# A retention and mixture-of-experts kernel: the first nine chunks computed whole instead of in halves

## The chip, the cores and the metric

The kernel runs on one core of a Trainium2 chip. The metric is the device time of one execution in microseconds (us); the median of three runs of the kernel before is 444.45 us (443.77 to 444.71). The first matrix dimension of a tile lies on up to 128 partitions. TensorE multiplies (PE in the profile, its weight loads PEld), VectorE (DVE) and ScalarE (ACT) work elementwise and read TensorE's result banks, GpSimd (POOL) makes some elementwise products and scatters rows by index, and SyncE (SP) issues most transfers.

## The reference

There are two stages. Retention takes q, k and v of 4 batches, 8 heads, 768 steps and 64 features. The result y is then regarded as 3072 tokens of 512 features, and each token goes to one of 8 experts:

```python
for t in range(S):
    state = gamma * state + einsum('bhd,bhe->bhde', k[:, :, t], v[:, :, t])
    y[:, :, t] = scale * einsum('bhd,bhde->bhe', q[:, :, t], state)
...
logits = x @ w_gate + modality_bias[modality_id]
e_idx = argmax(logits, axis=1)
...
h = maximum(x[mask] @ w1[e], 0.0)
out[mask] = gate_w[mask, None] * (h @ w2[e])
```

Each expert has w1 of 512 x 1024 and w2 of 1024 x 512. All data are float32.

## The kernel before, in words

*Chunks.* Retention works on 24 chunks of 128 tokens, `n` = 0 to 23, six for each batch. The growth of gamma is put into v ahead of time (`decay_v`, on GpSimd, makes the tile vd) and into the result afterwards (`gain`), so that a chunk needs four groups of matmuls: scores (sc, k times q), a masked copy of them on VectorE (a), the growth of the state (st, k times vd, which adds up in one bank over a batch) with a copy of the state by ScalarE (s), and the result y, which is state times q and a times vd. All are plain float32, and the trace shows two records for each such matmul.

*Halves.* Each chunk is worked in two halves of 64 tokens, with 8 heads, so that every operand is 64 x 64 and four matmuls lie in the four quarters of TensorE's array. `scores`, `heads_out` and `grown` make lists of matmuls, `run` issues two lists turn by turn, two matmuls of each, and `quarters(n)` puts them in order: the second half of chunk n's state and chunk n+1's scores beside chunk n's y, with one `yield` in the middle. The v and k of a chunk are laid out for this on the host (`toks`), and so are the factors `dec`.

*Tokens.* ScalarE copies y into yT. One chunk later `tokens_out` turns it and multiplies it with the gate's weights in one group of matmuls (x, 128 x 144), and VectorE and ScalarE make token rows (xs) and logits of it. Every three chunks are a group. `route` puts a group's steps into the list `todo`: choosing experts (`route_a`, which ends in cnt and crep), counting ranks (pc and rk on TensorE), then the scatter of the rows into x_dram by GpSimd. For some groups, the first of them group 1 (chunks 3 to 5), further steps (pk, pt) make a list of two jobs, each a full slot of 256 rows of one expert. Group 0 gives a guess of the first expert (totg), whose weights are loaded ahead.

*The order.* `everything` drives all this. Each time that the generator `retention` yields, `tick` issues one step of `todo`. In before a chunk yields twice. Once the first list exists, the rows and weights of the first job are loaded (the weights only if the guess was wrong), and a counter `ahead` runs down with the yields. When it is 1, the rows are flipped (xp, `flip_x`, with xTh and xTl as high and low parts) and the first quarter of w1 is split into hi (ScalarE, a cast) and lo (VectorE, a difference) by `cut`; at 0 the second quarter is split, and the jobs begin in the middle of chunk 9. From there on `run_job` issues the matmuls of the jobs (h_e with w1, o_e with w2, in three products of high and low parts) and takes a piece of retention at every third step. That part of the order is the same in both kernels.

*The engines' queues.* The order on TensorE, ScalarE, VectorE and SyncE is the order in which the program is written. An instruction that waits holds up all behind it on its engine.

Of the kernel before, what the change touches and what calls it, by code (L numbers as in the profile page):

```python
# [7 lines left out]
F32 = mybir.dt.float32  # L8
# [4 lines left out]
ALU = mybir.AluOpType  # L13
AX = mybir.AxisListType

P = 128
# [5 lines left out]
GRP = 3  # L22
# [11 lines left out]
UNIT = 32  # L34
NTAIL = 2
NUNIT = 144
DENSE = 9
EMPTY = 2 * NCAND
ZROW = NE * NT

# [3 lines left out]
FC = DF // P  # L44
QW = KC * 256

C_ID, C_MASK, C_DEC, C_IOTA, C_OUT, C_HALF, C_END = 0, 128, 256, 304, 312, 360, 424


@with_exitstack  # L50
def kernel(
# [23 lines left out]
    def bank(name):  # L75
        return ps.tile([P, 512], F32, tag="bank", name=name)
# [42 lines left out]

    gain = cst[:, C_OUT : C_OUT + NCH * H].rearrange("p (c h) -> p c h", h=H)  # L120
    half = cst[:, C_HALF : C_HALF + D]

    tbias = cp.tile([P, NN, NE], F32, name="tbias")
    iota3 = cp.tile([P, GRP, NE], F32, name="iota3")
# [139 lines left out]

    def quarters(n):
        more = 0 <= n and (n + 1) % NCH
        ys = []
        if n >= 0:  # L270
            py = bank(f"y_{n}").rearrange("p (g t) -> p g t", g=NG)
            ys = heads_out(n, py)
# [10 lines left out]
        if n >= 0:  # L283
            yield n
# [6 lines left out]
        if n < 0:  # L291
            return None
# [5 lines left out]
        nc.scalar.copy(yT, py)  # L298
        return yT
# [599 lines left out]
    def flip_x(s):  # L899
        s["xT"] = transpose_x(s["tag"], s["xg"])  # L900
# [43 lines left out]

    def decay_v(n):
        vv = kvs[n][:, 1].rearrange("p (h e) -> p h e", h=H)
        vds[n] = wk.tile([P, H, D], F32, tag="vd", name=f"vd_{n}", bufs=3)
        ins = nc.gpsimd.tensor_tensor(  # L948
            vds[n], vv, dec[:, n % NCH].unsqueeze(2).to_broadcast([P, H, D]), op=ALU.mult
        )  # L950
        vd_last[:] = [getattr(ins, "ins", ins)]

# [60 lines left out]
                todo.extend([lambda e=e: pad_c(e) for e in range(NE)])  # L1013

    def retention(modi):
        list(quarters(-1))
        masked(0)
        decay_v(1)
        setup_a()
        prev = None  # L1020
        for n in range(NN):
            yT = yield from quarters(n)
            if n + 1 < NN:
                masked(n + 1)
            if n + 2 < NN:
                decay_v(n + 2)

            load_kv(n + 7 if n < 3 else n + 3)
            load_kq(n + 8 if n < 4 else n + 4)
            if n == 0:  # L1030
                setup_b(modi)
            elif n == 1:
                list_consts()
            if prev is not None:
                tokens_out(*prev)
                if n % GRP == 0:
                    route(n // GRP - 1)
            prev = (n, yT)
            if n in (GRP - 1, (min(EVENTS) + 1) * GRP - 1):

                tokens_out(*prev)
                route(n // GRP)
                prev = None
            yield n
        tokens_out(*prev)
        route(NGRP - 1)
        yield NN

    def everything():
        load_kq(1)  # L1050
        load_kv(1)
        nc.sync.dma_start(wgt[:, :, P:], wgate)
# [12 lines left out]

        ahead = guess = None
        for n in ret:
            tick()
            if guess is None and "guess" in lists:
                guess = dict(e=reg(lists["guess"], 0, NE - 1))  # L1070
                raw(guess, 1)
                raw(guess, 2)
            if ahead is None:
                if min(EVENTS) in lists:
                    job = state_of[0] = start_job(jobs[0])
                    rows_in(job)
                    raw(job, 1, guess)
                    raw(job, 2, guess)
                    ahead = 2 * (DENSE - n)
            else:  # L1080
                ahead -= 1
                if ahead == 1:
                    flip_x(job)
                    cut(job, 1, 0)
                if ahead == 0:
                    cut(job, 1, 1)
                    break
        for k in range(len(jobs)):
            for t, _ in enumerate(run_job(k)):
                if t % 2:  # L1090
                    tick()
                if t % 3 == 1:
                    next(ret, None)
                if (k, t) in steps:
                    u = steps[k, t]
                    if u not in units:
                        at = 3 * NFIN + u
                        lst = lists["final"]
                        units[u] = unit(
                            f"u{u}", reg(lst, at + U, NE - 1), reg(lst, at, NCAND * UPS)  # L1100
                        )
                    next(units[u], None)
        assert next(ret, None) is None and not todo
# [18 lines left out]
def _layout(inputs):  # L1122
    import numpy as np

    f = np.float32
    q, k, v = inputs["q"], inputs["k"], inputs["v"]

    def feat(a):
        a = a.transpose(0, 1, 3, 2).reshape(B, NG, P, NCH, P)
        return a.transpose(0, 3, 2, 1, 4).reshape(NN, P, DM)  # L1130

    def toks(a):

        a = a.reshape(B, NG, 2, NCH, 2, D, D).transpose(0, 3, 2, 5, 4, 1, 6)
        return a.reshape(NN, P, DM)
# [7 lines left out]
    cst[:, C_DEC : C_DEC + NCH * H] = dec.reshape(P, NCH * H)  # L1143
    cst[:, C_IOTA : C_IOTA + NE] = np.arange(NE)
# [6 lines left out]
    cst[:, C_HALF:] = np.tile(np.triu(np.ones((D, D))), (2, 1))  # L1151
# [25 lines left out]
    return {n: np.ascontiguousarray(a) for n, a in arrs.items()}  # L1177
# [35 lines left out]
```

## Time and profile before

| | |
|---|---|
| median of three runs | 444.45 us (443.77 to 444.71) |
| the profiled execution | 440.58 us |
| its span, first to last instruction | 438.5 us |
| mean granted clock of TensorE | 0.967 |
| instructions | 13128 |
| TensorE busy | 402.6 us, 92% of the span, 5156 matmul records |
| VectorE, ScalarE, GpSimd busy | 242.8, 208.1, 101.9 us |
| moved by DMA | 92.83 MB, mean 212 GB/s |

A line of the timeline gives the start in us, the length in us, engine, line, operation and tiles, the count of merged records, and in brackets the idle time before it with what ended it. Lines of waits give the total, the number of times and the longest. Lines of windows give a stretch, its length, the busy us of each engine with its count, the granted clock, the share of the DMA engines and GB/s. "issue" means that the engine waited for nothing that the profile shows. The profiled execution lies 3.87 us below the median of the runs.

### The profile page before, as it was taken

How to read it: one execution, taken by the hardware profiler on the slowest of the kernel's cores; microseconds unless marked ns; L12 is line 12 of the kernel's file. 1: busy time of each engine (PE TensorE's matmuls, PEld its weight loads, DVE VectorE, ACT ScalarE, POOL GpSimd, SP SyncE). 2: the span in 40 equal slices, each digit the busy share in tenths (PEclk: the TensorE clock that was granted, in tenths of full speed). 3: DMA queues.
4: the chain of work that ended last, by engine and by line, in shares of the span. 5: the costliest groups of instructions: out<-in, count | busy, mean ns of one | idle time of the engine just before them, and what ended most of it. 6: DMA issues, size and time to landing. Idle time of an engine off the chain costs nothing.

```text
span 438.5 us, 13128 instructions
## 1 busy us (share of the span) xinstructions
PE 402.6 (92%) x5156; PEld 352.2 (80%) x5156; DVE 242.8 (55%) x581; ACT 208.1 (47%) x419; POOL 101.9 (23%) x130
## 2 busy tenths in 40 slices
PE   3777788999999998999999999999999999999990
PEld 3766677878988987988888988989898898869850
DVE  1452738756656647745754765887565664635400
ACT  1331436636447555446445636645454646445310
POOL 2423312152132024021311131030486101001010
PEclk9885989999999999999999999999999999999996
DMA  8999639985967682345770224662253999995000
GB/s 287 384 386 301 218 118 305 357 271 207 323 209 243 230 314 90 116 162 178 245 277 25 76 77 165 217 194 73 92 175 117 338 343 356 332 400 222 2 24 20
DMA packets 30895, 92.83 MB, mean 212 GB/s; under 512 B 5550, under 2 KB 5678, under 8 KB 30832
## 3 DMA queue, kind: packets, MB, share of 16 engines
q1 hardware_dynamic: 25360, 77.83, 51.4%
q0 software_dynamic: 5184, 13.67, 8.3%
q8 instruction: 41, 0.67, 0.7%
q10 hardware_dynamic: 288, 0.48, 0.3%
q14 instruction: 22, 0.18, 0.1%
HBM read 94.81 MB, written 17.21 MB: 255 GB/s over the span
## 4 chain that ended last, share of the span: by engine, by line
PE 58%; issue 14%; DMA 3%; DVE 3%; ACT 2%; POOL 2%; SPq 1%; POOLq 0%; ACTq 0%
PE o_e L784 21%; PE h_e L769 21%; PE x L308 4%; PE h_s L769 3%; PE sc L263 3%; PE st L263 2%; PE y L263 2%; DVE lo_e L715 2%; DMA wa_u<-in_w_dram 2%; PE xp_e L754 1%; DMA kq<-in_qkv_dram 1%; ACT hi_e L713 1%; POOL out_dram L797 1%; DMA xg_e<-x_dram 1%; PE uh_u L838 0%
## 5 line engine op out<-in xcount | busy, mean ns | idle before, releaser
L715 DVE TENSOR_TENSOR lo_e<-raw,hi_e 128x1024 fp32r<-128x1024 f32 x80 | 99.3, 1241 | 70.1 <-ACT hi_e L713 64.9
L769 PE MATMUL h_e<-xTh,hi_e 128*128 128x256 f32 x320 | 92.2, 288 | 0.9 <-ACT hi_e L713 0.9
L769 PE MATMUL h_e<-xTh,lo_e 128*128 128x256 f32 x320 | 90.5, 283 | 0.9 <-DVE lo_e L715 0.9
L769 PE MATMUL h_e<-xTl,hi_e 128*128 128x256 f32 x320 | 90.5, 283 | 0.0
L713 ACT CAST hi_e<-raw 128x1024 fp32r<-128x1024 f32 x80 | 83.8, 1047 | 0.0
L784 PE MATMUL o_e<-hi_e,hTh 128*128 128x512 f32 x160 | 66.2, 414 | 0.0
L784 PE MATMUL o_e<-lo_e,hTh 128*128 128x512 f32 x160 | 63.3, 396 | 0.0
L784 PE MATMUL o_e<-hi_e,hTl 128*128 128x512 f32 x160 | 63.1, 394 | 0.0
L769 PEld LDWEIGHTS h_e<-xTh,hi_e 128*128 128x128 f32 x320 | 61.2, 191 | 1.9 <-ACT hi_e L713 1.1
L769 PEld LDWEIGHTS h_e<-xTh,lo_e 128*128 128x128 f32 x320 | 61.2, 191 | 1.4 <-DVE lo_e L715 1.1
L769 PEld LDWEIGHTS h_e<-xTl,hi_e 128*128 128x128 f32 x320 | 61.2, 191 | 0.0
L948 POOL TENSOR_TENSOR vd<-kv,cst 128x512 f32<-128x512 f32 x24 | 26.8, 1117 | 115.6 <-PE y L263 54.8
L722 ACT ACTIVATE hTh<-h_e 128x256 fp32r<-128x256 f32 x80 | 30.5, 387 | 35.3 <-PE h_e L769 30.0
L263 PE MATMUL sc<-kq 64*64 64x64 f32 x768 | 37.4, 239 | 9.0 <-DMA kq<-in_qkv_dram 5.3
L723 DVE SCALAR_TENSOR_TENSOR hTl<-h_e,hTh 128x256 fp32r<-128x256 f32 x80 | 33.2, 419 | 21.1 <-ACT hTh L722 19.8
L258 ACT COPY s<-st 128x256 f32<-128x256 f32 x44 | 16.5, 375 | 58.4 <-PE y L263 31.2
L797 POOL DMA_INDIRECT out_dram<-o_e,xg_e x20 | 20.7, 1035 | 92.1 <-ACT o_e L796 86.2
L263 PEld LDWEIGHTS sc<-kq 64*64 64x64 f32 x768 | 30.7, 149 | 11.0 <-DMA kq<-in_qkv_dram 5.3
L330 ACT ACTIVATE xs<-x,cst 128x64 f32<-128x64 f32 x96 | 22.2, 315 | 33.9 <-issue 24.6
L414 POOL DMA_INDIRECT x_dram<-xs,pos x24 | 25.6, 1067 | 49.2 <-DVE xs L380 22.2
L263 PE MATMUL st<-vd,kv 64*64 64x64 f32 x704 | 33.3, 240 | 3.2 <-ACT s L258 1.1
L784 PEld LDWEIGHTS o_e<-lo_e,hTh 128*128 128x128 f32 x160 | 30.1, 188 | 7.3 <-DVE lo_e L715 0.3
(181 smaller groups left out, 707.0 us busy)
## 6 DMA issues: line engine op xcount, KB each, us to landing
raw<-in_w_dram SPq DMA_DIRECT2D x104, 512.0 KB
kv<-in_qkv_dram SPq DMA_DIRECT2D x24, 512.0 KB
kq<-in_qkv_dram SPq DMA_DIRECT2D x23, 512.0 KB
xg_e<-x_dram SPq DMA_DIRECT2D x20, 257.0 KB
wa_u<-in_w_dram SPq DMA_DIRECT2D x8, 512.0 KB
wb_u<-in_w_dram SPq DMA_DIRECT2D x16, 256.0 KB
xg_s<-x_dram SPq DMA_DIRECT2D x4, 257.0 KB
x_dram<-xs,pos POOLq DMA_INDIRECT x24
```

The costliest lines, as they stand in the source:

```text
L263: nc.tensor.matmul(out_, l, r, start=start, stop=True, skip_group_check=True)
L308: nc.tensor.matmul(px[:, g], yT[:, 2 * u + g], wgt[:, 2 * u + g], start=(g == 0), stop=(g == 1), skip_group_check=True,)
L330: nc.scalar.activation(x[:, i], px[:, i // 2, rows(i % 2)], AF.Copy, scale=gain[:, c, 4 * u + i : 4 * u + i + 1],)
L414: ins = nc.gpsimd.indirect_dma_start(out=x_dram[:, :], out_offset=bass.IndirectOffsetOnAxis(ap=pos[:, i : i + 1], axis=0), in_=xs, in_offs ...
L713: nc.scalar.copy(hi, raws[m][i])
L715: nc.vector.tensor_tensor(lo, raws[m][i], hi.bitcast(F32), op=ALU.subtract)
L722: nc.scalar.activation(hi, src, AF.Relu)
L723: nc.vector.scalar_tensor_tensor(lo, src, 0.0, hi.bitcast(F32), op0=ALU.max, op1=ALU.subtract)
L769: nc.tensor.matmul(ph, s["w1"][f // 2][wi][:, o : o + P], s["xT"][kc // 2][a][:, kc % 2, :], start=(n == 0), stop=(n == 3 * KC - 1),)
L784: nc.tensor.matmul(po, hT[f][a][:, hh * P : (hh + 1) * P], s["w2"][f // 2][wi][:, (f % 2) * DM : (f % 2 + 1) * DM], start=(n == 0), stop=( ...
L797: ins = nc.gpsimd.indirect_dma_start(out=out[:, :], out_offset=bass.IndirectOffsetOnAxis(ap=xg.bitcast(I32)[:, DM : DM + 1], axis=0), in_= ...
L948: ins = nc.gpsimd.tensor_tensor(vds[n], vv, dec[:, n % NCH].unsqueeze(2).to_broadcast([P, H, D]), op=ALU.mult)
```

## The change

For chunks 0 to 8 (`WHOLE = 9`) a chunk isn't halved. `whole_scores` makes 128 x 128 scores for each head, two at a time from the two halves of the partitions, into two banks, with two masks of 128 x 512 each. `whole_state` makes one group of 8 matmuls over 128 tokens, with one copy of the state. `whole_out` makes y 128 columns wide, 8 matmuls of state times q (none in a batch's first chunk) and 8 of a times vd. That is 32 matmuls for 64. Chunk 9 and later are as before, with other layouts of k, v and factors on either side of the border (`decw`, `whole`).

Within such a chunk there are now four yields, so four steps of `todo`: behind the state, behind the next chunk's scores, behind the tokens of the chunk before, and at the end. The counter `ahead` starts at 10 yields. The first quarter of w1 is split at 3, the second at 1 ahead of the flips. The loads of k and v stand earlier in a chunk.

```diff
+    def whole_scores(n):
+        for g in range(NG):
+            for j in range(2):
+                nc.tensor.matmul(
+                    p[j][:, g], kt[rows(j), g], qt[rows(j), g], start=True, stop=True,
...
+        for j in range(2):
+            nc.vector.tensor_tensor(
+                att[n][:, j], p[j], mask.unsqueeze(1).to_broadcast([P, NG, P]), op=ALU.mult
...
+    def whole_state(n):
+        for g in range(NG):
+            for j in range(2):
+                nc.tensor.matmul(
+                    p[rows(j), g], kk[:, 2 * g + j], vds[n][:, 2 * g + j],
...
+        keep_state(n + 1, 0)
...
+    def whole_out(n):
+        if s is not None:
+            for g in range(NG):
+                for j in range(2):
+                    nc.tensor.matmul(
+                        py[rows(1 - j), g], s[rows(j), g], qt[rows(j), g], start=(g == 0),
...
+        for g in range(NG):
+            for j in range(2):
+                nc.tensor.matmul(
+                    py[rows(1 - j), g], vd[:, 2 * g + j], a[:, j, g],
...
         for n in range(NN):
-            yT = yield from quarters(n)
-            if n + 1 < NN:
-                masked(n + 1)
+            if n < WHOLE:
+                if (n + 1) % NCH:
+                    whole_state(n)
+                load_kv(n + 7 if n < 3 else n + 3)
+                yield n
+                if n + 1 < WHOLE:
+                    whole_scores(n + 1)
+                else:
+                    first_halves(n + 1)
+                yield n
+                if prev is not None:
+                    tokens_out(*prev)
+                    if n % GRP == 0:
+                        route(n // GRP - 1)
+                    prev = None
+                yield n
+                yT = whole_out(n)
+            else:
+                yT = yield from quarters(n)
...
-                    ahead = 2 * (DENSE - n)
+                    ahead = AHEAD
             else:
                 ahead -= 1
+                if ahead == 3:
+                    cut(job, 1, 0)
                 if ahead == 1:
+                    cut(job, 1, 1)
                     flip_x(job)
-                    cut(job, 1, 0)
                 if ahead == 0:
-                    cut(job, 1, 1)
                     break
```

The first place is TensorE's queue around the tokens of chunk 5, where the first list begins. Here x is the turned y, st the state, pc and rk the ranks, crep the repeated counts. Before:

```order
L308 MATMUL x_1_835<-wgt,yT_806 128x144 x2
L263 MATMUL st_779<-vd_726,kv_143 64x64 x2
L263 MATMUL y_861<-kq_141,s_6_804 64x64 x2
L263 MATMUL st_779<-vd_726,kv_143 64x64 x2
L263 MATMUL y_861<-kq_141,s_6_804 64x64 x2
L263 MATMUL st_779<-vd_726,kv_143 64x64 x2
```

and, after more of the same and eight rows of scores and y by turns:

```order
L263 MATMUL sc_862<-kq_145 64x64 x2
L263 MATMUL y_861<-a_808,vd_726 64x64 x2
L548 LDWEIGHTS crep
L548 MATMUL pc_897<-ones,crep 96x1
L385 LDWEIGHTS upper
L385 MATMUL rk_907<-oh_854,upper 128x24
```

After the change, the whole way from x to rk:

```order
L367 MATMUL x_1_626<-wgt,yT_615 128x144 x2
L294 MATMUL st_652<-vd_567,kv_143 64x64 x8
L607 LDWEIGHTS crep
L607 MATMUL pc_663<-ones,crep 96x1
L444 LDWEIGHTS upper
L444 MATMUL rk_673<-oh_645,upper 128x24
```

In before 32 matmuls stand between x and pc; now only chunk 6's eight for the state do. Further on, 24 matmuls stood between rk and pk and 32 between pk and pt; now the eight scores of chunk 7 and none.

The second place is ScalarE's queue ahead of the first expert, where s is a copy of the state, yT a copy of y, xTh the high part of the flipped rows, and hi_e that of a quarter of w1 (raw_102 the first, raw_103 the second). Before:

```order
L258 COPY s_9_1192<-st_779 128x256
L298 COPY yT_1194<-y_1124 128x512
L330 ACTIVATE xs_1204<-x_1_1211,cst 128x64 x4
L727 CAST xTh_1225<-xp_e_1220 128x512
L727 CAST xTh_1234<-xp_e_1229 128x512
L713 CAST hi_e_1238<-raw_102 128x1024
L258 COPY s_10_1260<-st_779 128x256
L713 CAST hi_e_1278<-raw_103 128x1024
```

After:

```order
L262 COPY s_9_889<-st_652 128x256
L772 CAST hi_e_893<-raw_102 128x1024
L389 ACTIVATE xs_897<-x_1_904,cst 128x64 x4
L319 COPY yT_930<-y_913 128x512
L772 CAST hi_e_936<-raw_103 128x1024
L786 CAST xTh_945<-xp_e_940 128x512
L786 CAST xTh_954<-xp_e_949 128x512
L262 COPY s_10_976<-st_652 128x256
```

Both parts of w1 have moved ahead of the flipped rows.

More of the change, by code (lines that the diff above doesn't have):

```diff
@@ L36 @@
 NUNIT = 144
-DENSE = 9
+AHEAD = 10
+WHOLE = 9
 EMPTY = 2 * NCAND
@@ L45 @@
 QW = KC * 256
-C_ID, C_MASK, C_DEC, C_IOTA, C_OUT, C_HALF, C_END = 0, 128, 256, 304, 312, 360, 424
+C_ID, C_MASK, C_DEC, C_IOTA, C_OUT, C_HALF, C_DECW, C_END = 0, 128, 256, 304, 312, 360, 424, 472
 @with_exitstack
@@ L121 @@
     half = cst[:, C_HALF : C_HALF + D]
+    decw = cst[:, C_DECW : C_DECW + NCH * H].rearrange("p (c h) -> p c h", h=H)
     tbias = cp.tile([P, NN, NE], F32, name="tbias")
@@ L263, in run @@
                 nc.tensor.matmul(out_, l, r, start=start, stop=True, skip_group_check=True)
-    def quarters(n):
[L268 to L272, printed above, removed]
+    def whole_scores(n):
+        kt, qt = feat(n, 0), feat(n, 1)
+        p = [bank(f"sc{j}_{n}").rearrange("p (g t) -> p g t", g=NG) for j in range(2)]
+        for g in range(NG):
+            for j in range(2):
+                nc.tensor.matmul(
+                    p[j][:, g], kt[rows(j), g], qt[rows(j), g], start=True, stop=True,
+                    skip_group_check=True,
+                )
+        att[n] = me.tile([P, 2, NG, P], F32, tag=f"hi1{2 + n % 2}", name=f"a_{n}")
+        for j in range(2):
+            nc.vector.tensor_tensor(
+                att[n][:, j], p[j], mask.unsqueeze(1).to_broadcast([P, NG, P]), op=ALU.mult
+            )
@@ new lines, in whole_state @@
+    def whole_state(n):
+        c = n % NCH
+        if c == 0:
+            pst[n // NCH] = bank(f"st_{n}")[:, : NG * D].rearrange("p (g e) -> p g e", g=NG)
+        p = pst[n // NCH]
+        kk = kvs[n][:, 0].rearrange("p (h d) -> p h d", h=H)
+        for g in range(NG):
+            for j in range(2):
+                nc.tensor.matmul(
+                    p[rows(j), g], kk[:, 2 * g + j], vds[n][:, 2 * g + j],
+                    start=(c == 0 and g == 0), stop=True, skip_group_check=True,
+                )
+        keep_state(n + 1, 0)
+        if c == NCH - 2 and n + 1 < WHOLE:
+            pst.pop(n // NCH)
@@ new lines, in whole_out @@
+    def whole_out(n):
+        py = bank(f"y_{n}").rearrange("p (g t) -> p g t", g=NG)
+        qt, a, vd, s = feat(n, 1), att.pop(n), vds.pop(n), sts.pop((n, 0), None)
+        if s is not None:
[3 more added lines that the diff above has]
+                        py[rows(1 - j), g], s[rows(j), g], qt[rows(j), g], start=(g == 0),
+                        stop=True, skip_group_check=True,
+                    )
+        for g in range(NG):
+            for j in range(2):
+                nc.tensor.matmul(
+                    py[rows(1 - j), g], vd[:, 2 * g + j], a[:, j, g],
+                    start=(s is None and g == 0), stop=True, skip_group_check=True,
+                )
+        yT = wk.tile([P, NG, P], F32, tag="yT", name=f"yT_{n}")
+        nc.scalar.copy(yT, py)
+        return yT
@@ L273, in quarters, with first_halves @@
+    def first_halves(n):
+        run(scores(n))
+        run(grown(n, 0))
+        keep_state(n, 1)
+        masked(n)
+    def quarters(n):
+        more = (n + 1) % NCH
+        py = bank(f"y_{n}").rearrange("p (g t) -> p g t", g=NG)
+        ys = heads_out(n, py)
         own = grown(n, 1) if more else []
@@ L290, in quarters @@
             run(ys[k:])
-        if n < 0:
-            return None
         for u in range(2):
@@ L946, in decay_v @@
         vv = kvs[n][:, 1].rearrange("p (h e) -> p h e", h=H)
+        by = decw if n < WHOLE else dec
         vds[n] = wk.tile([P, H, D], F32, tag="vd", name=f"vd_{n}", bufs=3)
         ins = nc.gpsimd.tensor_tensor(
-            vds[n], vv, dec[:, n % NCH].unsqueeze(2).to_broadcast([P, H, D]), op=ALU.mult
+            vds[n], vv, by[:, n % NCH].unsqueeze(2).to_broadcast([P, H, D]), op=ALU.mult
         )
@@ L1015, in retention @@
     def retention(modi):
-        list(quarters(-1))
-        masked(0)
+        whole_scores(0)
         decay_v(1)
@@ L1021, in retention @@
         for n in range(NN):
-            yT = yield from quarters(n)
-            if n + 1 < NN:
-                masked(n + 1)
+            if n < WHOLE:
[13 more added lines that the diff above has]
+                    prev = None
+                yield n
+                yT = whole_out(n)
+            else:
+                yT = yield from quarters(n)
+                if n + 1 < NN:
+                    masked(n + 1)
+                load_kv(n + 3)
             if n + 2 < NN:
                 decay_v(n + 2)
-            load_kv(n + 7 if n < 3 else n + 3)
             load_kq(n + 8 if n < 4 else n + 4)
@@ L1130, in feat, with whole @@
         return a.transpose(0, 3, 2, 1, 4).reshape(NN, P, DM)
+    def whole(a):
+        return a.transpose(0, 2, 1, 3).reshape(NN, P, DM)[:WHOLE]
     def toks(a):
+        w = whole(a)
         a = a.reshape(B, NG, 2, NCH, 2, D, D).transpose(0, 3, 2, 5, 4, 1, 6)
-        return a.reshape(NN, P, DM)
+        return np.concatenate([w, a.reshape(NN, P, DM)[WHOLE:]])
     gam = 1.0 - 2.0 ** (-5.0 - np.arange(H, dtype=np.float64))
@@ L1143, in _layout @@
     cst[:, C_DEC : C_DEC + NCH * H] = dec.reshape(P, NCH * H)
+    dec = (gam[None, :] ** (-t[:, None])).reshape(NCH, P, H)
+    cst[:, C_DECW:] = dec.transpose(1, 0, 2).reshape(P, NCH * H)
     cst[:, C_IOTA : C_IOTA + NE] = np.arange(NE)
@@ L1150, in _layout @@
     cst[:, C_OUT : C_OUT + NCH * H] = gain.transpose(1, 0, 2).reshape(P, NCH * H)
-    cst[:, C_HALF:] = np.tile(np.triu(np.ones((D, D))), (2, 1))
+    cst[:, C_HALF : C_HALF + D] = np.tile(np.triu(np.ones((D, D))), (2, 1))
     ci = np.arange(NCAND)
```

2 lines of the change are left out of this document (removed).

## The prediction

> **What bounds the kernel now.** I read the page's chain first, then the busy time of two stretches, then who keeps TensorE waiting in the first.
>
> ```profile
> PE 58%; issue 14%; DMA 3%; DVE 3%; ACT 2%; POOL 2%; SPq 1%; POOLq 0%; ACTq 0%
> ```
>
> ```profile
> 8.30:68.60 60.30, 46.67 (x1274) 41.10 (x1274) 28.05 (x115) 21.82 (x66) 17.24 (x30) 0.83 0.80 283
> 68.60:438.50 369.90, 353.95 (x3850) 309.27 (x3850) 213.77 (x466) 184.96 (x352) 83.13 (x94) 0.99 0.57 199
> ```
>
> The columns are the stretch, its length, then busy us of PE, PEld, DVE, ACT and POOL, the clock, the DMA share and GB/s. From 68.6 us on, where the first expert's matmuls run, TensorE is busy for 354.0 of 369.9 us at a clock of 0.99. The change leaves the order there alone, so an earlier or later start of the first expert should come through to the end one to one. The term to forecast is the start of that stretch, and before it TensorE is busy for only 46.7 of 60.3 us. Its waits up to there:
>
> ```profile
> PE y L263 <- issue: 5.6, 8, 1.5
> PE sc L263 <- DMA kq<-in_qkv_dram: 5.3, 1, 5.3
> PE sc L263 <- issue: 3.0, 4, 1.9
> ...
> PE pc L548 <- DVE crep L543: 0.8, 1, 0.8
> ```
>
> Most of the waiting after the first load is "issue": TensorE waited for nothing that the trace shows. Four of these stand in the timeline, in the middle of runs of matmuls whose operands were there; behind them is TensorE's busy time and count of records from each to the next:
>
> ```profile
> 16.55 0.27 PE L263 MATMUL y<-kq,s 64*64 64x64 f32 x1 [1.37 <-issue]
> ...
> 23.02 0.27 PE L263 MATMUL y<-kq,s 64*64 64x64 f32 x2 [1.50 <-issue]
> ...
> 29.21 0.21 PE L263 MATMUL sc<-kq 64*64 64x64 f32 x1 [1.93 <-issue]
> ...
> 34.22 0.37 PE L263 MATMUL y<-kq,s 64*64 64x64 f32 x2 [1.07 <-issue]
> ```
>
> ```profile
> 16.55:23.02 6.47, 4.97 (x128) 0.74 1.02 372
> 23.02:29.21 6.19, 4.27 (x126) 1.00 1.03 411
> 29.21:34.22 5.01, 3.88 (x128) 0.62 0.86 320
> ```
>
> ```profile
> q8 instruction: 41, 0.67, 0.7%
> ```
>
> The stalls come every 126 to 128 matmul records. 41 packets of instructions make 5156 records / 41 = 126 each, so each stall is TensorE at the end of a packet whose successor isn't there. A packet took 5.0 to 6.5 us, mean 5.9. A float32 matmul is two records here (768 score records over 24 chunks are 32, for 16 matmuls), so a chunk is 128 records and 8 for x: 136, or 1.07 packets. This part runs at the rate of instruction supply, some 6.3 us a chunk, not at TensorE's rate. The stalls have a second cost:
>
> ```profile
> 16.80:20.20 3.40, 3.40 (x73) 3.28 (x64) 1.72 (x10) 0.86 (x2) 1.89 (x2) 0.50 1.03 406
> 30.46:44.11 13.65, 11.39 (x269) 9.89 (x265) 4.37 (x20) 3.02 (x9) 5.25 (x6) 0.50 0.94 303
> ```
>
> After the stall of 1.37 us the clock is 0.50 for 3.40 us, after that of 1.93 for 13.65, four times as long. Over 8.3 to 68.6 the 0.83 above makes (1 - 0.83) x 2 x 60.3 = 20.5 us of half clock.
>
> **The change part by part.** *Records.* A whole chunk has 32 matmuls for 64: 64 records, and 8 for x: 72. At 5.9 us per 127 its supply takes 3.3 us. That is less than TensorE's own time, as the next step shows, so these stalls should go, and TensorE's own time is late next.
>
> *TensorE's own time.* Prices at full clock, at half clock, and of one width against another:
>
> ```profile
> 14.19 0.22 PE L263 MATMUL st<-vd,kv 64*64 64x64 f32 x2
> ...
> 14.48 0.23 PE L263 MATMUL st<-vd,kv 64*64 64x64 f32 x2
> ...
> 24.12 0.28 PE L263 MATMUL y<-a,vd 64*64 64x64 f32 x3
> 24.33 2.24 PE L308 MATMUL x<-wgt,yT 128*128 128x144 f32 x16
> 26.50 0.27 PE L263 MATMUL st<-vd,kv 64*64 64x64 f32 x2
> ...
> 32.30 0.32 PE L263 MATMUL st<-vd,kv 64*64 64x64 f32 x2
> ...
> 32.73 0.32 PE L263 MATMUL st<-vd,kv 64*64 64x64 f32 x2
> ```
>
> ```profile
> 5.26 1.97 PE L263 MATMUL sc<-kq 64*64 64x64 f32 x32 [5.26 <-DMA kq<-in_qkv_dram]
> ```
>
> A set of four records, one in each quarter of the array, steps by (14.48 - 14.19) / 5 = 0.058 us, at half clock by (32.73 - 32.30) / 4 = 0.108. So 128 records a chunk were 1.86 us. The lone scores at 5.26, two quarters at a time and at half clock, step by 1.97 / 16 = 0.12 a pair: two at a time cost as much per step as four. The new forms fill the array with two, and their length goes with the columns: 64 columns 0.058 a pair, 128 columns twice that, 0.115 (the x records, 144 columns, are 2.17 / 16 = 0.136 each). A chunk: scores 8 x 0.115 = 0.92, state 8 x 0.058 = 0.46, y 16 x 0.115 = 1.84, together 3.22, and x 1.0. Against before that is 1.36 us more work per chunk.
>
> Before shows no 64x128 or 128x64 form, so what each switch of form costs is an estimate. Going from quarters to whole, the last set starts at 24.12 + 0.058 = 24.18 and x at 24.33, 0.15 later where a set takes 0.058: 0.09 over, and more lies hidden in the x records. I take 0.15, between 0.09 and 0.2. A chunk before has two switches (into x and out), a whole one four (into scores, x, state times q, and a times v; the next state has the form just used). I take four, and two as the cheap end, 0.3 less a chunk. [...] A full chunk is 3.22 + 1.0 + 0.6 = 4.8 us at full clock.
>
> *The first list.* Its steps follow one another by a quarter of a chunk, and TensorE has less to do between them:
>
> ```profile
> 28.64 0.17 DVE L371 TENSOR_TENSOR cnt<-cnt,new 128x8 bf16<-128x8 bf16 x1
> ```
>
> ```profile
> 44.89 1.86 PE L308 MATMUL x<-wgt,yT 128*128 128x144 f32 x13
> ```
>
> ```profile
> 49.39 0.21 DVE L543 COPY crep<-cnt 128x96 bf16<-128x96 bf16 x1
> ...
> 52.29 0.67 DVE L208 TENSOR_TENSOR a<-sc,cst 128x512 f32<-128x512 f32 x1
> ...
> 53.57 0.47 DVE L611 TENSOR_SCALAR ohs<-ord_r,rank,full 96x2 bf16<-96x2 f32 x1
> ```
>
> From the end of x to cnt VectorE needs 28.81 - 26.57 = 2.24 us, to crep 49.60 - 46.75 = 2.85, and from a mask's start to ohs 54.04 - 52.29 = 1.75, with a second mask now 2.4. Behind x of chunk 5 only the state (0.6) is left ahead of pc, so TensorE waits some 2.2 us there (0.8 before). Behind the scores of chunk 7 only pk is left ahead of pt: 2.1 us. In chunk 3 totg waits 1.6 for cnt. Queued behind each on TensorE are the rest of that chunk's matmuls. The same steps reach the list of the first job some 11 us ahead of its rows' flips, so rows and weights come in under two chunks of matmuls.
>
> *The start of the first expert.*
>
> ```profile
> 64.02 1.34 PE L754 MATMUL xp_e<-cst,xg_e 128*128 128x128 f32 x8
> ```
>
> ```profile
> 67.38 0.38 PE L769 MATMUL h_e<-xTh,hi_e 128*128 128x256 f32 x1 [0.94 <-ACT hi_e L713]
> 68.64 0.39 PE L769 MATMUL h_e<-xTh,lo_e 128*128 128x256 f32 x1 [0.88 <-DVE lo_e L715]
> ```
>
> ```profile
> 65.93 1.29 DVE L728 TENSOR_TENSOR xTl<-xp_e,xTh 128x512 fp32r<-128x512 f32 x2 [1.22 <-ACT xTh L727]
> ```
>
> ```profile
> 24.67 0.59 ACT L298 COPY yT<-y 128x512 f32<-128x512 f32 x1
> ...
> 66.24 1.09 ACT L713 CAST hi_e<-raw 128x1024 fp32r<-128x1024 f32 x1
> ```
>
> The waits of 0.94 and 0.88 go. Late next are xTh and xTl: ahead of xTh on ScalarE now stand yT of chunk 8 (0.59) and hi of the second quarter (1.09), so the cover is only the flips and half a chunk.
>
> *Sum.* vd is ready at 8.25:
>
> ```profile
> 7.21 1.04 POOL L948 TENSOR_TENSOR vd<-kv,cst 128x512 f32<-128x512 f32 x1 [6.12 <-DMA cst<-in_consts_dram]
> ```
>
> Chunk 0, still at half clock (5.26's step), takes 4.7 to 13.0; chunks 1 and 2 4.8 each: 22.6; yT and x of chunk 2 1.8: 24.4; chunk 3 with its wait 6.4: 30.8; chunk 4 4.8, chunk 5 without a state 4.2: 39.8; yT and x 1.8: 41.6; chunk 6 with two waits 8.7: 50.3; chunk 7 4.8: 55.1; chunk 8 with the first halves of chunk 9 5.7: 60.8; flips 1.1 and half a chunk 1.1: 63.0; the last of xT about 64.2 (60.8 + 0.6 + 1.0 + 1.1 + 0.7), of which h_e's own first records hide half: 63.6. Against 68.6 this is 5.0 us earlier.
>
> Two losses. The half clock: it came in stretches of 3.4 us, and chunk 6's two waits lie within 5 us, each longer than the 1.93 that lowered the clock. Two stretches, 6.8 us, less 2.1 of waiting, at half speed lose 2.3 us. [...] And slow issue beside a scatter of token rows:
>
> ```profile
> 34.01 1.15 POOL L414 DMA_INDIRECT x_dram<-xs,pos  x1 [1.25 <-ACT s L258]
> ```
>
> ```profile
> 36.06 0.35 PE L263 MATMUL sc<-kq 64*64 64x64 f32 x1 [0.29 <-issue]
> ...
> 36.80 0.26 PE L263 MATMUL y<-a,vd 64*64 64x64 f32 x1 [0.26 <-issue]
> ```
>
> For some three us after a scatter begins TensorE starts a few records each 0.74 us, where a whole chunk would start 0.74 / 0.058 = 13. That costs between 0 (if something else waits then) and 2.2 a time; I take 1.1, once, since the second scatter lies beside chunk 6's wait. So 5.0 - 2.3 - 1.1 = 1.6 us earlier. ScalarE saves 9 copies, VectorE does 9 masks more (0.67 each, 6 us of some 32 idle there); both are hidden behind TensorE, except where counted.
>
> **The rivals.** *The clock stays up* and the scatter costs nothing: 5.0 earlier. For: the waits may fall on either side of a stretch's border. Against: 1.37 to 1.93 us were enough before. [...] 440.58 - 5.0 = 435.6 by the profiled execution, 439.4 by the median.
>
> *New waits become the bound (slower).* Chunk 3's wait (1.6) lowers the clock as well, 1.7; the second scatter costs 1.1; a switch is 0.2, so 36 x 0.05 = 1.8. That is 4.6 on top: 3.0 later, 447.4. It decides from about 1.6 us more than my losses. For: TensorE now has 1.36 us more work a chunk, so nothing covers a miss. Against: the 8.6 us of issue waits above are a gain that none of this touches.
>
> *They cancel*: within 0.9 us (0.2%, about what a measurement of this kernel can tell).
>
> *Pairs don't overlap.* If the new forms ran one at a time, 3.2 us more a chunk over nearly nine: about 27 later, 471. Against: the pairs at 5.26.
>
> **How the numbers follow.** The profiled execution took 440.58 us, with a span of 438.5; the median of the runs is 444.45, 3.87 above it, and I carry the difference over: 444.45 - 1.6 = 442.9 (alone: 441.0 to 443.5). Chances: this forecast 0.27, clock up 0.19, cancel 0.18, new waits 0.32, no overlap 0.04. Faster 0.46, same 0.18, slower 0.36. The range reaches 1.2 us past the two middle rivals: 438.2 to 448.6.
>
> **What would show it.** Right: no issue wait of 1 us or more every 127 records before the first h_e; 72 records a chunk at near 4.8 us; waits of some 2 us at totg, pc and pt; half clock around chunk 6 alone; the first steady h_e near 67.0. Wrong: issue stalls that stay; pairs that step by more than 0.13; h_e that waits over 1.5 us for xTl; a stretch behind h_e whose length differs by over 1 us from 369.9.

## The result and the profile after

The changed kernel took 440.12 us (median of 20 runs, 439.00 to 444.69), the kernel before beside it 444.01 (20 runs, 442.48 to 446.75). The ratio is 0.993, with a 95% interval of 0.9906 to 0.9954. The medians lie 3.9 us apart and the means 3.0, since four of the changed kernel's runs took 444.05 to 444.69, at a mean clock of 0.972 for 0.975 to 0.982 in the others. A second, later comparison gave 0.9965 (0.9931 to 0.9998, before at 443.55). So the change makes the kernel faster, by something between 0.1 and 4.2 us; the forecast was 1.6.

The profiled executions took 440.58 us (span 438.5) before and 439.6 (span 437.5) after. The windows of the changed kernel's trace, up to the first steady h_e and from there on:

```profile
8.30:67.00 58.70, 49.23 (x715) 43.14 (x715) 33.06 (x124) 18.73 (x57) 19.79 (x32) 0.94 0.85 308
67.00:437.50 370.50, 354.75 (x3849) 310.08 (x3849) 212.60 (x466) 185.34 (x352) 81.78 (x93) 0.98 0.57 196
```

The first stretch is 1.6 us shorter (58.70 for 60.30). TensorE's busy time in it rose by 2.6 (49.23 for 46.67), with 715 records for 1274, and its waiting fell by 4.2 (9.5 for 13.6). At a clock of 0.94 for 0.83, half clock fell from 20.5 us to 0.06 x 2 x 58.7 = 7.0. What TensorE waited for there:

```profile
PE sc L276 <- DMA kq<-in_qkv_dram: 5.3, 1, 5.3
PE pt L680 <- DVE ohs L670: 2.5, 1, 2.5
PE pc L607 <- DVE crep L602: 1.9, 1, 1.9
PE totg L643 <- DVE cnt L430: 1.7, 1, 1.7
PE x L367 <- ACT yT L319: 1.5, 2, 0.7
PE h_e L828 <- ACT xTh L786: 0.9, 1, 0.9
PE st L294 <- POOL vd L1008: 0.9, 1, 0.9
```

No line says "issue" any more. Before, three did, with 9.6 us in all; the prediction shows two, and this is the third:

```profile
PE st L263 <- issue: 1.0, 2, 0.7
```

In their place stand the list's steps: pt, pc and totg, 6.1 us together. The page's packets of instructions and its chain:

```profile
q8 instruction: 36, 0.59, 0.5%
...
PE 57%; issue 26%; POOL 5%; DVE 5%; DMA 3%; ACT 2%; POOLq 0%; ACTq 0%
```

There are 36 packets for 41. The "issue" of the chain, 26% (14% before), lies elsewhere: of its 112 us some 99 stand behind 298 us. In another trace of the same kernel the chain's share is 8%, so it says little about the change.

### The profile page after: what moved, and what is told of

Its sections match the earlier page's. It is cut to its first block, busy times and chain, and to the rows that moved or that the text cites. A ratio compares the mean times of both kernels' runs of the same rounds, so it can differ in the third digit from the quotient of the medians.

```text
span 437.5 us, 11969 instructions
## 1 busy us (share of the span) xinstructions
PE 406.1 (93%) x4580; PEld 355.0 (81%) x4580; DVE 246.5 (56%) x590; ACT 205.4 (47%) x410; POOL 103.1 (24%) x130
## 4 chain that ended last, share of the span: by engine, by line
PE 57%; issue 26%; POOL 5%; DVE 5%; DMA 3%; ACT 2%; POOLq 0%; ACTq 0%
PE h_e L828 17%; PE o_e L843 17%; PE x L367 6%; PE sc L267 3%; PE st L267 3%; PE y L314 2%; PE sc L276 2%; PE y L267 2%; POOL out_dram L856 2%; POOL x_dram L533 2%; DVE lo_e L774 1%; PE y L308 1%; DMA cst<-in_consts_dram 1%; PE xp_e L813 1%; ACT hi_e L772 1%
## 5 line engine op out<-in xcount | busy, mean ns | idle before, releaser
L1008 POOL TENSOR_TENSOR vd<-kv,cst 128x512 f32<-128x512 f32 x24 | 28.2, 1174 | 102.1 <-PE y L267 51.2
L782 DVE SCALAR_TENSOR_TENSOR hTl<-h_e,hTh 128x256 fp32r<-128x256 f32 x80 | 33.3, 420 | 21.8 <-ACT hTh L781 20.5
L843 PEld LDWEIGHTS o_e<-hi_e,hTh 128*128 128x128 f32 x160 | 30.1, 188 | 5.9
L843 PEld LDWEIGHTS o_e<-hi_e,hTl 128*128 128x128 f32 x160 | 30.2, 189 | 5.4
L855 ACT ACTIVATE o_e<-o_e,xg_e 128x512 f32<-128x512 f32 x20 | 13.8, 691 | 39.0 <-issue 24.8
L367 PE MATMUL x<-wgt,yT 128*128 128x144 f32 x192 | 30.0, 299 | 1.5 <-ACT yT L319 1.5
```

The costliest lines, as they stand in the source:

```text
L367: nc.tensor.matmul(px[:, g], yT[:, 2 * u + g], wgt[:, 2 * u + g], start=(g == 0), stop=(g == 1), skip_group_check=True,)
L782: nc.vector.scalar_tensor_tensor(lo, src, 0.0, hi.bitcast(F32), op0=ALU.max, op1=ALU.subtract)
L843: nc.tensor.matmul(po, hT[f][a][:, hh * P : (hh + 1) * P], s["w2"][f // 2][wi][:, (f % 2) * DM : (f % 2 + 1) * DM], start=(n == 0), stop=( ...
L1008: ins = nc.gpsimd.tensor_tensor(vds[n], vv, by[:, n % NCH].unsqueeze(2).to_broadcast([P, H, D]), op=ALU.mult)
```

## The experiments

Each ratio is to the kernel before, run on the same chip beside it, with its 95% interval. Three theories were held against each other. *Supply*, the prediction's: fewer records a chunk end the waits for instructions ("issue" waits at the ends of packets, called supply waits here). *Steps*: the gain comes from the first list's steps a quarter of a chunk apart. *Cuts*: it comes from hi and lo of w1 made ahead of the flips.

**One part alone: the steps.**

```diff
+            if 0 <= n < DENSE:
+                yield n
...
-                    ahead = 2 * (DENSE - n)
+                    ahead = 10
```

> The kernel before (quarters in all chunks, its own order of flips and cuts) with a step of the list behind each quarter of a chunk in the first nine chunks, as in the changed kernel. Supply: 136 records a chunk stay, so the issue waits stay (at least five of 1 us or more before the first h_e); new waits of 1 to 2 us at totg and pt take the place of some of them; first steady h_e 67 to 70, the time 443 to 446 (before: 444.0). Steps: the gain comes with the steps alone, first steady h_e 67 or earlier, the time 441 or less.

Measured: 1.0014 (0.9981 to 1.0046), the first steady h_e at 70.3. The waits of TensorE up to there:

```profile
PE y L263 <- issue: 8.9, 3, 4.4
PE sc L263 <- DMA kq<-in_qkv_dram: 5.2, 1, 5.2
...
PE totg L593 <- DVE cnt L380: 1.7, 1, 1.7
```

The supply waits are there in full (fewer and longer than expected), and the list's waits come on top. The steps alone bring nothing.

**One part undone: the cuts.**

```diff
-                if ahead == 3:
-                    cut(job, 1, 0)
                 if ahead == 1:
-                    cut(job, 1, 1)
                     flip_x(job)
+                    cut(job, 1, 0)
                 if ahead == 0:
+                    cut(job, 1, 1)
```

> The changed kernel with the order of before at its end: flips first, then the first quarter of w1 made into hi and lo, the second quarter half a chunk later. Supply: h_e waits for hi and lo instead of xTh and xTl, by 0 to 1 us more: first steady h_e 67.0 to 68.2, the time 440 to 441.3. Cuts: the whole gain goes, 443 to 444.5.

Measured: 0.9955 (0.9925 to 0.9985). The gain isn't gone. Whether the cuts are worth a us this can't tell: the interval covers both of the changed kernel's ratios. In its trace h_e waited 1.5 us, for hi and lo, where it waits 1.9 for xTh and xTl in the changed kernel: the expected "0 to 1 us more" didn't show.

**One part undone: the steps.**

```diff
-AHEAD = 10
+AHEAD = 7
...
-            todo.extend([a1, b, c, d])
+            todo.extend([a1, wait, b, wait, c, wait, d])
...
-            todo.extend([a1, guess_a, b, c])
+            todo.extend([a1, wait, guess_a, wait, b, wait, c])
```

> The changed kernel with the steps of the first list, and of the guess ahead of it, half a chunk apart as before instead of a quarter (the list one step list[1] comes three quarters of a chunk later in the order). Supply: the waits of TensorE at totg, pc and pt (1.7 + 1.9 + 2.5 = 6.1 us) fall below 3 in sum and the half clock between 47 and 54 us goes; late next are the scatters and with them the token rows of the first job, for which the flips (xp) then wait up to 3 us. First steady h_e 63 to 67, the time 437 to 440.5. Steps: without the earlier list the gain goes; first steady h_e 69 or later, the time 442.5 or more.

Measured: 0.9925 (0.9894 to 0.9956), the first steady h_e at 64.8. Its waits:

```profile
PE h_e L828 <- ACT xTh L786: 1.7, 1, 1.7
PE pk L629 <- DVE rkt L456: 1.6, 1, 1.6
...
PE h_e L828 <- DVE xTl L787: 0.9, 1, 0.9
PE pc L607 <- DVE crep L602: 0.8, 1, 0.8
```

The gain is kept, so it doesn't come from the steps. totg (0.6) and pc wait less and pt no more, as expected, but pk now waits 1.6, which was not, and h_e waits 2.6 for 1.9: for the flips' results, not for the token rows. The half clock did not go either: it now stood from 45.6 to 52.4, and began inside the wait at pk.

**The whole chunks alone**, with both of the last two edits:

> Only the whole chunks of the change: the steps of the first list half a chunk apart and the order of flips and cuts as before. Supply (the gain came because fewer records a chunk ended the waits for instructions): no issue waits of 1 us or more before the first h_e, and the gain is there with nothing else of the change: ratio to before 0.990 to 0.997. Steps and Cuts (the gain needs the list's steps or the cuts): 1.000 or above, as the steps alone gave 1.0014.

Measured: 0.9861 (0.9810 to 0.9912), with no supply wait. The windows up to the first steady h_e and behind it:

```profile
8.39:63.89 55.50, 49.46 (x714) 42.68 (x714) 33.21 (x124) 19.05 (x57) 18.77 (x32) 0.94 0.89 319
63.89:431.30 367.41, 352.85 (x3850) 309.28 (x3850) 214.16 (x466) 185.24 (x352) 80.57 (x93) 0.99 0.57 198
```

The whole gain lies in the whole chunks: 0.9861 is below the expected 0.990 to 0.997, into which the interval reaches. The start is 2.1 to 3.2 us shorter than the changed kernel's (55.50 for 57.63 and 58.70 in its two traces). That the other two parts cost this much isn't shown, since the runs were made at different times and the interval overlaps that of the first comparison; that the gain needs neither is.

**More records, the first two attempts.** Each 128-column matmul of scores and y as two of 64 columns, and then every matmul of a whole chunk in two with the row halves taking turns:

```diff
-                    p[j][:, g], kt[rows(j), g], qt[rows(j), g], start=True, stop=True,
-                    skip_group_check=True,
+                    p[j][:, g, rows(w)], kt[rows(j), g], qt[rows(j), g, rows(w)],
+                    start=True, stop=True, skip_group_check=True,
```

> The changed kernel with each 128-column matmul of the scores and of y in whole chunks issued as two of 64 columns: the same products, columns and forms, but 120 records a chunk for 72. Supply (the gain came because fewer records a chunk ended the waits for instructions): 120 x 5.9 / 127 = 5.6 us a chunk against 4.8 of TensorE's own time, so issue waits of 1 us or more come back every 126 to 128 records, at least four before the first h_e; the first steady h_e moves from 67.0 to 70 to 74 and the time to 443 to 447. Steps and Cuts (the gain came from the list's steps a quarter of a chunk apart, or from hi and lo of w1 ahead of the flips): both are kept, so the first steady h_e stays within 1 us of 67.0 and the time within 1 us of the changed kernel's 440.1.

> The changed kernel with every matmul of the whole chunks (scores, state and y) cut in two by columns, the two row halves still taking turns: 136 records a chunk as before the change, the same products and forms. In the run with 120 records the two column halves of one row half stood one behind the other, a pair of 64 columns then stepped by 0.118 in the scores, and a chunk took over 6 us by TensorE's own time, so it tells nothing of supply. Supply: TensorE's own time a chunk is 4.8 plus at most 0.6, and 136 records at 5.9 per 127 want 6.3, so issue waits of about 1 us come back every 126 to 128 records, at least three before the first h_e; the time is 5 to 12 us above the changed kernel's, ratio to before 1.003 to 1.020. Rival (TensorE's own time is all that counts): no issue waits of 0.5 us or more, and the time rises by at most 9 x 0.6 = 5 us.

Measured: 1.0254 (1.0194 to 1.0314) and 1.0371 (1.0317 to 1.0426), and no supply wait in either. Both expectations failed. The scores of one chunk in the second of these kernels, then in the changed one:

```profile
23.81 2.00 PE L277 MATMUL sc<-kq 64*128 64x64 f32 x32
```

```profile
13.68 1.16 PE L276 MATMUL sc<-kq 64*128 64x128 f32 x16
```

Half the columns took nearly the same time each: 32 records from 23.81 to the x at 25.74, 0.060 us a record, where 16 took from 13.68 to 14.77, 0.068 a record. The weight loads of that stretch fit this:

```profile
23.81 1.86 PEld L277 LDWEIGHTS sc<-kq 64*128 64x128 f32 x32
```

A load of 128 weight columns takes 1.86 / 32 = 0.058 us, and there is one for each record. So a matmul of 64 columns, at 0.060, gained next to nothing behind it, and TensorE's own time rose: a chunk of the second kernel ran from 22.81 to 28.98, 6.2 us (4.8 in the changed kernel), at which 136 records ask for a packet only every 5.8 us. These kernels didn't put supply to the test. They show that TensorE's own time a chunk grew with records too, 6.2 us for 136 against 4.8 for 72, where each brought a load.

**Tiny records in two quarters.** 64 matmuls of 16 columns behind the scores:

```diff
+        for k in range(8):
+            for g in range(NG):
+                for j in range(2):
+                    nc.tensor.matmul(
+                        p[rows(j), k, g], kt[rows(j), g, :D], qt[rows(j), g, :16],
...
```

> The changed kernel with 64 more matmuls behind the scores of each of chunks 1 to 8: one quarter of the array each, 16 columns, into a bank that nobody reads. That is 128 records more, 200 a chunk, at no more than the 0.0145 us a record that quarters of 64 columns take (0.058 for four), so TensorE's own time is at most 4.8 + 1.9 + 0.15 = 6.9 us a chunk. Supply (a packet of 127 records comes at best every 5.0 to 6.5 us): 200 records want 7.9 to 10.2 us, so issue waits of 1 us or more come every 126 to 128 records, six or more before the first h_e, and the time rises by 8 x 3.1 to 8 x 5.4, less some 4 us of other waits that these overlap: 21 to 39 us, ratio to before 1.04 to 1.08. Rival (TensorE's own time is all that counts, and supply never held anything up): no issue waits of 0.5 us or more, and at most 8 x 2.1 = 17 us more: ratio 1.032 or less.

Measured: 1.1154 (1.1098 to 1.1210), one supply wait of 0.6. Both theories missed. The tiny records stepped by 0.030 us (128 from 34.65 to the x at 38.48), and their weight loads, 64 columns wide, took as long (3.29 us for 110 loads, nearly all of them theirs, in the first window of the last section), so a chunk took some 8.5 us and asked for a packet every 5.4. And the clock fell where nothing waited, as the last section shows.

**Tiny records in four quarters,** by which TensorE asks for more than supply can give:

```diff
+                for i in range(2):
+                    for j in range(2):
+                        nc.tensor.matmul(
+                            p[i][rows(j ^ i), k, g], kt[rows(j), g, :D], qt[rows(j), g, :16],
...
```

> The changed kernel with 128 tiny matmuls (256 records) behind the scores of each of chunks 1 to 8, in turn in all four quarters of the array, as the quarters of the kernel before were. With two quarters in turn the tiny records stepped by 0.029 us each, a chunk of 200 took 8.5 us by TensorE's own time, which is 5.4 per 127 records, and no supply wait came: that run only shows that a packet every 5.4 us can be had. In four quarters they should step by 0.0145, so that TensorE wants a packet every 127 x 0.0145 = 1.8 us among them and 3.4 over a chunk of 328 records (4.8 + 3.7 + 0.15 = 8.7 us of its own). Supply (a packet comes every 5.0 to 6.5 us at best): issue waits of 2 us or more every 126 to 128 records, at least eight before the first h_e, and 328 records take 12.9 to 16.8 us a chunk: 60 to 95 us above the changed kernel, ratio to before 1.13 to 1.21. Rival (supply never held anything up, TensorE's own time is all): no issue waits of 1 us or more, 8 x 3.9 = 31 us more, or 60 if these too step by 0.029, the runs of tiny records without a break.

Measured: 1.1529 (1.1460 to 1.1598). The wait line of the new matmuls, and the timeline around two of the waits:

```profile
PE tiny L295 <- issue: 13.8, 7, 3.7
```

```profile
24.88 2.04 PE L295 MATMUL tiny<-kq 64*64 64x16 f32 x125
30.56 3.85 PE L295 MATMUL tiny<-kq 64*64 64x16 f32 x131 [3.64 <-issue]
...
40.96 2.86 PE L295 MATMUL tiny<-kq 64*64 64x16 f32 x180
45.55 2.32 PE L295 MATMUL tiny<-kq 64*64 64x16 f32 x76 [1.73 <-issue]
```

The windows from one such wait to the next, with the count of records behind PE's busy time:

```profile
17.95:30.56 12.61, 8.97 (x256) 8.60 (x255) 1.29 (x2) 0.96 (x2) 1.04 (x1) 0.90 0.85 330
30.56:45.55 14.99, 13.26 (x384) 12.41 (x383) 2.93 (x13) 1.79 (x6) 1.28 (x4) 0.73 0.22 73
45.55:68.58 23.03, 16.83 (x382) 15.31 (x382) 5.52 (x23) 2.92 (x11) 1.12 (x2) 0.65 0.43 147
```

They lie 256, 384 and 382 records apart: two, three and three times 128. The supply waits are back in whole chunks, at the ends of packets, with nothing but records added. The time is in the expected range by another sum, though: the waits are 13.8 us in seven places, two of them over 2 us (eight or more were expected), the tiny records' own time is some 31 by the expectation's sum, and half clock takes much of the rest (0.74 from 8.4 us to the first steady h_e at 140.8).

**The clock in the list's waits.** Two matmuls of 472 columns, whose result nobody reads, in each of the waits at pc and pt:

```diff
+    def filler(nm):
+        pz = bank(nm)
+        for _ in range(2):
+            nc.tensor.matmul(pz[:, :C_END], ident, cst, start=True, stop=True)
...
+        if t == min(EVENTS):
+            filler("fill_a")
...
+        if g == min(EVENTS):
+            filler("fill_b")
```

> The changed kernel with two more matmuls of 472 columns, whose result nobody reads, ahead of pc and two ahead of pt, about 1.8 us in each of the two waits (1.9 and 2.5). If idle time inside the waits lowers the clock (my step on the half clock), the stretch of half clock between 47 and 54 us goes and 2 to 3 us with it, though TensorE has more to do: ratio to before 0.985 to 0.990. If the half clock has another cause, the stretch stays and the time is the changed kernel's or up to 1 us more: 0.992 to 0.996.

Measured: 0.9861 (0.9809 to 0.9913). The window up to the first steady h_e:

```profile
8.34:64.00 55.66, 49.72 (x724) 41.70 (x724) 32.81 (x124) 18.71 (x57) 17.37 (x31) 1.00 0.86 310
```

With more work for TensorE the stretch is 2.0 to 3.0 us shorter than the changed kernel's, at a clock of 1.00, though pt still waited 0.9. The half clock at pc and pt was the price of these waits. A shorter stretch behind the border, which a later section shows, is gone too, though h_e still waited 0.9 twice; why isn't shown.

**The waits taken away.**

```diff
-AHEAD = 10
+AHEAD = 8
...
-            todo.extend([a1, b, c, d])
+            todo.extend([a1, wait, b, wait, c, d])
...
+                if n == LATE:
+                    whole_masked(n)
...
-                if ahead == 3:
+                if ahead == 4:
                     cut(job, 1, 0)
+                if ahead == 2:
+                    flip_x(job)
                 if ahead == 1:
                     cut(job, 1, 1)
-                    flip_x(job)
...
```

> The changed kernel with its waits taken away: the guess's and the list's steps half a chunk apart up to pk, then pt a quarter later; chunk 7's two masks on VectorE behind the list's steps; the second group's scatters right behind its positions, and on GpSimd ahead of the next vd; the flips three quarters of a chunk, and the first cut one quarter, earlier. If the waits at totg, pc, pt and h_e (6.1 + 1.9 us) and the half clock around them hold back what the whole chunks save, the first steady h_e comes 3 to 6 us earlier than the changed kernel's and the ratio to before is 0.978 to 0.988. If another chain takes their place (the token rows of the first job, for which the flips would then wait), under 2 us earlier: 0.989 to 0.993.

Measured: 0.9854 (0.9806 to 0.9902), the first steady h_e at 64.0, 1.9 to 3.0 us ahead of the changed kernel's (3 to 6 were expected). pt waited 0.7, pc 0.8, h_e not at all, but the second case came true beside the first:

```profile
PE xp_e L820 <- DMA xg_e<-x_dram: 2.6, 2, 2.3
```

The token rows are late next, and the clock was at half from 58.8 to 62.2 behind that wait. Hence the last version, with flip and second cut a quarter later, and beside it the changed kernel once more:

> The run with the waits taken away, with the flips again a quarter of a chunk later, behind y of chunk 8, since TensorE there waited 2.3 us for the token rows with nothing in between and fell to half clock for 3.4 us behind it. If that wait and its half clock are what was left: xp waits under 0.7 us, h_e up to 1.5 us for xTh, the half clock between 58 and 62 us goes, the first steady h_e comes 0 to 2.5 us earlier than 64.0, ratio to before 0.979 to 0.985. If the wait only moves to h_e: 0.985 to 0.988.

> The changed kernel itself, on the chip of this call. Supply with its losses (the steps a quarter apart cost waits and half clock): a ratio to before of 0.990 to 0.996, above the 0.986 of the whole chunks alone and of the filled waits. If those two were lower by their chip alone, 0.983 to 0.988.

Measured: 0.9870 (0.9809 to 0.9932) for this version and 0.9965 (0.9931 to 0.9998) for the changed kernel on the same chip. The windows of the version's trace:

```profile
8.37:61.87 53.50, 47.22 (x716) 40.33 (x716) 31.92 (x123) 17.81 (x57) 18.31 (x31) 1.00 0.89 327
61.87:434.90 373.03, 355.79 (x3849) 309.75 (x3849) 213.00 (x467) 185.80 (x353) 81.06 (x93) 0.99 0.56 196
```

The start is as expected: 61.9, four us ahead of the changed kernel's 65.9 in its run beside it, at full clock. The ratio is above the expected 0.979 to 0.985: the rest of that execution took 373.0 for 370.8, so part of the gain was given back later; its trace shows 1.8 us of "issue" waits at h_e and o_e behind 75 us, which the changed kernel's traces lack, and half clock from 329.1 to 332.5. The changed kernel's 0.9965 is just above the expected 0.990 to 0.996 and far from 0.983 to 0.988, which the chip alone would have given; the chip of the runs at 0.986 wasn't tried.

By ratio the filled waits, these two versions and the whole chunks alone, 0.985 to 0.987, can't be told from one another, and they beat the kernel before. The last version is the one shown to beat the changed kernel too, side by side: medians of 435.83 (6 runs, 433.83 to 439.04) and 440.49 (12 runs, 438.74 to 447.77). The other three ran on another chip, without the changed kernel beside them.

## Why the prediction was right, point by point

**The supply waits go.** Right, and the cause is shown from three sides: they leave with whole chunks alone, stay with the steps alone, and come back when cheap records are added to whole chunks. The trace of before also dates the packets: they landed at 15.29, 21.92, 27.80 and 32.82 us, 1.1 to 1.4 us ahead of the ends of the four waits that the prediction shows. The price of "5.0 to 6.5 us a packet" held as a range: at a packet every 5.4 us a single wait of 0.6 came, and where TensorE asked for more, a packet took 6.3 and 5.0 us over the first two windows above. In before the 41 packets hold 0.67 MB, 16 KB each, and 128 records with a weight load each (5156 of either in the execution) are 256 instructions. What sets when a packet is fetched stays open.

The prediction counted all "issue" waits as supply, those beside a scatter too, and took the whole part ahead of h_e for bound by it. Of the 9.6 us, 6.9 are six waits at the ends of packets: the four that it shows, 0.29 at 47.90 and 0.69 at 53.09. So behind 34.22 us supply cost only 1.0. Another 2.5 are seven waits of 0.26 to 0.40 us beside the scatters or right behind them (36.06 to 37.56 and 55.08 to 57.35). The changed kernel shows none of these either; why they go isn't shown.

**TensorE's own time, 4.8 us a chunk.** Right. The changed kernel's chunks, from state to state (the second row from chunk 2's state, the third in chunk 4, beside the first scatters):

```profile
13.11:17.90 4.79, 4.79 (x76) 4.28 (x75) 4.65 (x20) 1.45 (x5) 1.94 (x2) 1.00 1.03 416
17.90:22.70 4.80, 4.80 (x76) 4.19 (x72) 2.43 (x9) 2.02 (x8) 1.28 (x4) 1.00 1.03 398
...
30.67:35.55 4.88, 4.88 (x77) 4.20 (x73) 2.50 (x9) 1.17 (x4) 3.38 (x4) 1.00 1.01 400
```

A chunk has 72 records; the windows also catch the ends of a few before. By the starts in the first window, scores took 1.09 us to the next group, x 1.18, y 1.02 and 0.92, the state 0.57. Over the prices without switches (0.92, 1.09, 0.92, 0.92, 0.46) that is a switch in four places, as taken, of 0.09 to 0.17 each: 0.47 in all for the 0.6 taken, while x alone is 1.09 for 1.0.

**The list's waits.** Right in place and sum: 1.7, 1.9 and 2.5 for 1.6, 2.2 and 2.1.

**The half clock around chunk 6.** Right: two stretches, as these windows show.

```profile
43.83:47.24 3.41, 1.94 (x24) 1.58 (x24) 2.79 (x16) 0.00 (x0) 0.00 (x0) 1.00 0.98 399
47.25:54.07 6.82, 5.13 (x52) 4.76 (x53) 2.04 (x10) 0.96 (x2) 4.03 (x4) 0.50 0.39 144
67.73:71.14 3.41, 3.41 (x19) 3.41 (x17) 1.22 (x2) 1.32 (x2) 0.00 (x0) 0.50 0.97 278
```

5.13 us busy at half speed lose 2.6, for 2.3 forecast, and the filled waits show the cause. In the first row, right ahead of the half clock, TensorE was busy for 1.94 of 3.41 us: the clock didn't stay up, as the first rival has it, though no wait there was longer than 2.5 us. The third row was not foreseen, and half clock was to stand around chunk 6 alone: behind the waits for xTh and xTl it cost another 1.7 past the border, part of why the rest took 370.5 for 369.9.

**The scatter's 1.1.** Wrong: 4.88 us for the chunk beside the first scatters leaves 0.1 of it.

**The start of the first expert.** 67.0, as forecast, but by luck: two errors of 1.8 us cancel. The flips began at 62.4, where the sum with its losses gives 60.8 + 2.3 + 1.1 = 64.2; the scatter cost 1.0 less, chunks 6 to 8 with their half clock took 1.0 less, and what stands ahead of chunk 6 took 0.2 more. From there to the first steady h_e it took 4.6 us, for 2.8 forecast. ScalarE and VectorE show why:

```profile
62.60 0.93 ACT L389 ACTIVATE xs<-x,cst 128x64 f32<-128x64 f32 x4 [1.87 <-DVE lh L375]
63.40 0.60 ACT L319 COPY yT<-y 128x512 f32<-128x512 f32 x1
...
64.98 1.38 DVE L774 TENSOR_TENSOR lo_e<-raw,hi_e 128x1024 fp32r<-128x1024 f32 x1 [2.16 <-ACT hi_e L772]
66.28 1.28 DVE L787 TENSOR_TENSOR xTl<-xp_e,xTh 128x512 fp32r<-128x512 f32 x2
...
67.02 0.39 PE L828 MATMUL h_e<-xTl,hi_e 128*128 128x256 f32 x1 [1.02 <-DVE xTl L787]
```

The token rows xs stand ahead of yT on ScalarE, and lo of the second quarter ahead of xTl on VectorE. The forecast's sum for the last of xT (yT, hi, xTh, xTl) has neither.

**The sum.** By the profiled executions 1.6 us earlier at the border and 1.0 at the end; by the first comparison's ratio some 3.1, by the second's 1.5. The profiled execution of before, 440.58, lies under all 20 of its timed runs, so carrying its distance to the median, 3.87, over was the weak step: it put the forecast at 442.9 for 440.12 measured. The changed kernel's profiled execution lies only 0.5 under its median. What the other executions of before lose more isn't shown.

## What to carry to other kernels

Where "issue" waits come every fixed number of records (126 to 128 here), count records and not columns: wider matmuls that are no better by array time can win (here 72 records a chunk for 136 ended them, at 1.36 us more work a chunk by the prediction's sum), until a load per record (0.058 us for 128 weight columns here) or the array itself (4.8 us a chunk here) is the bound. What that frees is soon taken by the next chain, here the list's steps on VectorE; a wait there may cost half as much again in half clock (2.6 us for 4.4 at pc and pt), and a few useless wide matmuls in it can be cheaper than the wait (here the stretch up to h_e was 2.0 to 3.0 us shorter with them).

## What the runs showed of the hardware that was not expected

*The clock fell without a wait.* In the kernel with tiny records in two quarters the clock fell behind a window without a gap:

```profile
22.55:25.96 3.41, 3.41 (x114) 3.29 (x110) 1.29 (x2) 0.00 (x0) 0.00 (x0) 1.00 1.03 401
25.96:29.38 3.42, 3.42 (x38) 3.24 (x34) 0.52 (x2) 0.00 (x0) 0.00 (x0) 0.50 0.75 298
```

TensorE was busy throughout, nearly all of it with 16-column matmuls. Half clock came in steps of 3.41 us: in the changed kernel from 47.25 to 54.07, two steps, and from 67.73 to 71.14, one, with 20.48 us, six steps, from start to start. The same wait of 1.7 at totg stood ahead of half clock in one kernel and not in another, and it fell differently in the steps. In the changed kernel it began in one step and ended in the next:

```profile
23.35:26.76 3.41, 1.86 (x24) 1.58 (x24) 2.10 (x11) 1.59 (x7) 0.77 (x2) 1.00 1.02 412
26.76:30.17 3.41, 3.04 (x46) 2.67 (x48) 2.81 (x13) 0.00 (x0) 0.00 (x0) 1.00 1.04 413
```

In the kernel with tiny records in four quarters it lay inside one:

```profile
55.32:58.73 3.41, 1.72 (x44) 1.45 (x39) 2.64 (x15) 1.35 (x6) 0.00 (x0) 1.00 0.03 7
58.73:62.14 3.41, 3.32 (x129) 3.21 (x125) 1.17 (x2) 0.00 (x0) 0.00 (x0) 0.50 0.43 118
```

Busy time alone doesn't sort these rows: half clock followed steps that were busy for 1.72, 1.94 (around chunk 6) and 3.41 us, and none followed the one of 1.86. What exactly is counted stays open.

*VectorE slow beside GpSimd.* With the steps spread, one small sum of two tensors took 1.00 us for its usual 0.15 (the row of the changed kernel stands last):

```profile
44.47 1.00 DVE L621 TENSOR_TENSOR key<-key,first_g 96x1 f32<-96x1 f32 x1
```

```profile
44.42 1.04 POOL L1008 TENSOR_TENSOR vd<-kv,cst 128x512 f32<-128x512 f32 x1 [5.07 <-issue]
```

```profile
45.45 0.15 DVE L621 TENSOR_TENSOR key<-key,first_g 96x1 f32<-96x1 f32 x1
```

It ended with GpSimd's vd beside it, and pk, which waited 1.6 us in that kernel, is made from this sum. It isn't alone: in the changed kernel, key<-size,cnd took 0.41 to 0.51 us beside such a product in three places (87.26, 168.43 and 210.33), each time ending within 0.01 us of it, and 0.15 to 0.16 elsewhere. lh<-x,cst, which reads one of its operands from TensorE's result banks, took its usual 0.18 to 0.19 there. What holds VectorE there isn't shown.
